# Attention by sketched features, then a Fourier mixer: rows divided as 34c + t, contiguous loads of q, features stationary in k-v, and a new order

## The chip, the cores and the metric

The kernel runs on one core of one Trainium2 chip. Its engines are TensorE (PE, matrix products), VectorE (DVE), ScalarE (ACT), GpSimd (POOL) and SyncE (SP, which here issues the loads and stores). The metric is the device time of one execution in microseconds (us); lower is better. Beside it stands the span of the profiled execution, from its first to its last instruction.

## The reference, cut to what matters

There are 4 batches, 4 heads, 1088 rows, 32 numbers a head. Each row of q and k is turned into 64 features: two projections to 8 numbers each, and all products of the two.

```python
def phi(x):                       # S1, S2: 8 x 32
    a = einsum('rd,bhsd->bhsr', S1, x)
    b = einsum('rd,bhsd->bhsr', S2, x)
    return (a[..., :, None] * b[..., None, :]).reshape(*x.shape[:-1], 64)
q_p, k_p = phi(q), phi(k)
kv = einsum('bhsf,bhsd->bhfd', k_p, v)
z = k_p.sum(axis=2)
x = einsum('bhsf,bhfd->bhsd', q_p, kv) / (einsum('bhsf,bhf->bhs', q_p, z)[..., None] + 1e-6)
x = x.transpose(0, 2, 1, 3).reshape(4, 1088, 128)
mixed = real(fft(fft(x, axis=1), axis=2))
u = x + mixed
un = (u - mean(u)) / sqrt(var(u) + 1e-6)
out = u + maximum(un @ w_ch1, 0) @ w_ch2          # w_ch1: 128 x 512, w_ch2: 512 x 128
```

## The kernel before, in words

The program is a list of named steps. Each step has the engines that may run it, what it reads and writes, and the PSUM banks that it uses. A text, ORDER, gives the order in which the steps are emitted; every engine works its own instructions in that order. ENGINE names the engine of a step that has a choice, and BANK gives the PSUM bank (of eight, 512 float32 columns each) of each use. An entry such as `7@0` in ORDER stands for seven products of a zero tile into bank 0, whose results nobody reads; the text calls them filler products (line 734). There is no scheduler at run time: a step that waits holds up what stands behind it on its engine.

Per batch b the steps are these.

- `ld_k`, `ld_v`, `ld_q`: the loads, issued on SP. k comes as 34 rows a partition, contiguous (4352 bytes); q comes in four loads of 128 KB each, in which a partition gets two neighbouring rows of all four heads (runs of 256 bytes). The 64 rows of a batch that do not fit this pattern come for all batches in five small loads (`ld_qt`).
- `kT`, `kpr`, `kab`, `kp`: k is transposed in 32x32 blocks on VectorE (line 318), projected on TensorE (line 308), copied out of PSUM, and multiplied to features, mostly on POOL (line 77). `kt_pr`, `kt_a`, `kt_p` do the same for the last tile.
- `vc`, `vl`: v is copied beside a column of ones, so that one product gives kv and z.
- `kv`, `kvt`: k-v on TensorE (line 357). v with its ones, 33 columns, is the stationary operand, and the 64 features stream. The result is 33 x 64 a head. `kvc` copies it to SBUF, `kvr` turns it by four products with an identity (line 369), and `kvz` puts it into place as 64 x 33.
- `qT`, `qf`, `qa`, `qp`: q is transposed (line 408) and projected straight to 64 repeated columns of each projection by 16 products of 32 x 64 with 256 columns (line 415). `qa` copies one of the two results (ScalarE, line 70), and `qp` multiplies the two (VectorE, line 426). A step works half a batch and takes four PSUM banks. `qt_T`, `qt_f` (line 437), `qt_a`, `qt_p` do it once for the left-over rows of all batches.
- `pnd`, `den`, `x`: numerator and denominator (line 460), reciprocal, quotient.
- `fo`, `eo`: sums and differences of the two halves and of even and odd parts of x (line 77, on VectorE or POOL).
- `sC`, `sS`: the transform along the rows by products with cosine and sine tables (lines 488 and 492); `zC`, `zS` copy the result out, and `zrC`, `zrS` store it reversed.
- `mix`, `bn`, `sd`, `rc`, `un`, `tr`, `ut`, `ph`, `rl`, `po`, `fin`, `out`: for each half batch g, the transform along the 128 columns, the normalization, a transposition, the two products of the mixer with the relu between them (lines 575 to 597), and the stores. Groups 4 and 9 hold the left-over rows of two batches each.

The tables are made on the chip (`c_iota`, `c_rows`, `c_last`, `t_turn`, `t_ph`, `t_pm`, `t_sin`, `t_cos`, and `t_m...` and `t_again`, which fill in the mirrored part). Batches go in the order 3, 2, 1, 0; the first k is loaded in two parts (`parts`, with `FIRST = 3`).

Of the kernel before, what the change touches and what calls it, by code (L numbers as in the profile page):

```python
# [10 lines left out]
FP32 = mybir.dt.float32  # L11
BF16 = mybir.dt.bfloat16
I32 = mybir.dt.int32
# [10 lines left out]
NM = HALF // 4 + 1  # L24
NF = HALF // 2 + 1
NK = NF + 17
# [27 lines left out]
def program(nc, T, x, bank):  # L54
# [48 lines left out]
    QUARTERS = (1, HALF + 1, S - 256, HALF - 256)  # L103

    def ld_q(b, w):
        nc.sync.dma_start(view(T(f"q_in{b}"), 2 * H * D * w, [[2 * D, H], [1, 2 * D]]),  # L106
                          dram(x["q"], (b * H * S + QUARTERS[w]) * D, [[2 * D, 128], [S * D, H], [1, 2 * D]]))


    def ld_qt(e):  # L110
        for p, n, row, step in ((0, 16, 257, 1), (16, 15, 273, 1), (32, 16, 801, 1), (48, 15, 817, 1)):
            nc.sync.dma_start(view(T("qt_in"), 0, [[D, B * H], [1, D]], p, n),  # L112
                              dram(x["q"], row * D, [[step * D, n], [S * D, B * H], [1, D]]))
        a = T("qt_in")[:]
        pitch = a.ap[0][0]
        nc.sync.dma_start(bass.AP(tensor=a.tensor, offset=a.offset + 31 * pitch, ap=[[32 * pitch, 2], [D, B * H], [1, D]]),
                          dram(x["q"], 0, [[HALF * D, 2], [S * D, B * H], [1, D]]))
    add("ld_qt", "SP", "", "qt_in", ld_qt)
    for b in range(B):
        for i, (lo, n) in enumerate(parts(b)):  # L120
            add(f"ld_k{b}.{i}", "SP", "", f"k_in:{b}/{i}", lambda e, b=b, n=n, lo=lo: ld_k(b, n, lo))
        add(f"ld_v{b}", "SP", "", f"v_in:{b}", lambda e, b=b: ld_v(b))
        for w in range(4):
            add(f"ld_q{b}.{w}", "SP", "", f"q_in:{b}/{w}", lambda e, b=b, w=w: ld_q(b, w))
# [12 lines left out]
    def c_iota(e):  # L137
        nc.gpsimd.iota(T("kk")[:], pattern=[[1, 2], [2, NM]], base=-1, channel_multiplier=0,
                       allow_small_or_imprecise_dtypes=True)
        nc.gpsimd.iota(T("pi")[:], pattern=[[0, 1]], base=0, channel_multiplier=1)  # L140
        nc.gpsimd.iota(T("sr")[:, 0:2], pattern=[[1, 2]], base=1, channel_multiplier=2,
                       allow_small_or_imprecise_dtypes=True)
# [4 lines left out]
    def c_rows(e):  # L147
        nc.vector.tensor_scalar(out=T("sq")[:, 0:2], in0=T("sr")[:, 0:2], scalar1=1.0 / S, scalar2=None, op0=ALU.mult)
# [4 lines left out]
    def c_last(e):  # L153
# [4 lines left out]
        pa, pf, row = T("pa"), T("pf"), T("sr")[:, 2:3]  # L158
        ts(pa[:, 0:1], T("pi")[:], 31, ALU.bitwise_and)
        ts(pa[:, 1:2], T("pi")[:], 32, ALU.bitwise_and)  # L160
        ts(pa[:, 2:3], T("pi")[:], 1, ALU.bitwise_and)
        ts(pf[:, 0:1], pa[:, 0:1], 31.0, ALU.is_equal, -288.0, ALU.mult)
        ts(pf[:, 1:2], pa[:, 0:1], 257.0, ALU.add, pf[:, 0:1], ALU.add)
        ts(row, pa[:, 1:2], HALF / 32.0, ALU.mult, pf[:, 1:2], ALU.add)
        ts(T("sq")[:, 2:3], row, 1.0 / S, ALU.mult)
        ts(T("sg")[:, 0:1], pa[:, 2:3], 2.0, ALU.mult, -1.0, ALU.add)
        ts(T("sg")[:, 1:2], pa[:, 2:3], -2.0, ALU.mult, 1.0, ALU.add)
    add("c_last", "DVE", "iota", "last", c_last)
# [35 lines left out]
    def mirror(e, at, step, n, sign):  # L204
        out = view(T("tab"), at * 2 * NK + NM, [[step * 2 * NK, n], [NK, 2], [1, NM - 1]])
        in_ = view(T("tab"), at * 2 * NK + NM - 1, [[step * 2 * NK, n], [NK - 1, 2], [-1, NM - 1]])
        if isinstance(sign, float) and sign == 1.0:
            copy(e, out, in_)
        elif e == "ACT":
# [12 lines left out]
    add("t_mP", "ACT DVE POOL", "tab:0/S tab:1/C", "tab:m/P", lambda e: mirror(e, 1, 1, 2, 1.0))  # L222
    add("t_mN", "ACT DVE POOL", "tab:0/C tab:1/S", "tab:m/N", lambda e: mirror(e, 0, 3, 2, -1.0))
# [584 lines left out]
```

## Time and profile before

| | us |
|---|---|
| median of 3 runs | 87.29 (86.96 to 87.42) |
| the profiled execution | 87.3 |
| its span | 85.5 |
| TensorE busy | 74.7 |
| VectorE busy | 68.1 |
| ScalarE busy | 55.6 |
| POOL busy | 40.5 |

A row of a group gives the line, the engine, the operation, what it writes and reads, the shape, a count, the busy time and the mean duration of one in ns. A row of a stretch gives the busy time and count of TensorE's products, TensorE's weight loads, VectorE, ScalarE and POOL, then the granted TensorE clock, the share of the DMA engines' time and GB/s. A row of the timeline gives the start, the time from the first start to the last end, and the instructions merged; `[1.24 <-DVE ...]` is idle time before it and what ended it. A float32 product shows as two records on TensorE. Durations of TensorE's products overlap, so the distance from start to start tells what a group holds the engine for. A tile's name stands for all its buffers; `t_k_in` also serves as the buffer of the outputs.

### The profile page before, as it was taken

What the parts mean: (1) busy time and instruction counts of PE and PEld (TensorE: products, weight loads), DVE (VectorE), ACT (ScalarE), POOL (GpSimd) and SP (SyncE); (2) the same over time, 40 slices, a digit from 0 to 9 for tenths busy, and PEclk for the clock granted to TensorE, in tenths of its full rate; (3) what the DMA queues carried; (4) which work ended last, traced back from release to release, by engine and by line L of the source; (5) the groups of instructions that cost most, each with busy time, mean ns of one, the idle gap of its engine ahead of it and who ended that gap; (6) DMA issues with size and microseconds to landing.
All of it is one profiled execution on the core that took longest, in us unless ns stands there. A gap on an engine that the chain in (4) does not pass through costs nothing.

```text
span 85.5 us, 3315 instructions
## 1 busy us (share of the span) xinstructions
PE 74.7 (87%) x1399; PEld 54.2 (63%) x1407; DVE 68.1 (80%) x139; ACT 55.6 (65%) x102; POOL 40.5 (47%) x69
## 2 busy tenths in 40 slices
PE   4999949799987999999999999699899998988800
PEld 1237517798855697846797888376478786855700
DVE  4769495999999759976999598999989889976300
ACT  2637799096915797675493656693768898875720
POOL 6889996069955996799900950360030000000000
PEclk9999999999999999999999999999999999999998
DMA  1896999969999810000000000000033122034061
GB/s 17 175 254 131 314 358 315 280 142 243 270 309 379 212 24 4 8 0 0 0 8 0 8 0 0 8 20 11 0 123 123 45 85 93 30 123 131 22 211 43
DMA packets 14942, 9.65 MB, mean 113 GB/s; under 512 B 10064, under 2 KB 13392, under 8 KB 14928
## 3 DMA queue, kind: packets, MB, share of 16 engines
q1 hardware_dynamic: 14848, 9.44, 39.0%
q8 instruction: 11, 0.18, 1.0%
q14 instruction: 3, 0.02, 0.1%
q10 hardware_dynamic: 80, 0.01, 0.1%
HBM read 7.22 MB, written 2.23 MB: 110 GB/s over the span
## 4 chain that ended last, share of the span: by engine, by line
PE 54%; DVE 18%; DMA 8%; SPq 7%; ACT 5%; issue 3%; ACTq 0%; DVEq 0%
PE ps L357 9%; DMA t_k_in__100<-in_k_dram 8%; PE ps L460 8%; PE ps L597 7%; PE ps L415 7%; PE ps L488 5%; PE ps L575 4%; PE ps L520 3%; PE ps L308 2%; SPq L106 2%; SPq L112 2%; DVE t_v__127 L72 2%; PE ps L492 2%; PE ps L567 2%; PE ps L514 2%
## 5 line engine op out<-in xcount | busy, mean ns | idle before, releaser
L734 PE MATMUL ps<-t_wz 128*128 128x512 bf16 x19 | 7.5, 530 | 1.2 <-DVE t_wz L130 1.2
L70 ACT COPY t_qa__128<-ps 128x1024 f32<-128x1024 f32 x4 | 4.0, 1012 | 4.1 <-PE ps L415 4.1
L734 PEld LDWEIGHTS <-t_wz 128*128 128x128 bf16 x22 | 2.3, 119 | 4.8 <-issue 3.0
L70 ACT COPY t_qa__129<-ps 128x1024 f32<-128x1024 f32 x4 | 4.1, 1013 | 1.2 <-PE ps L415 1.2
L575 PEld LDWEIGHTS <-t_w1b 128*128 128x128 bf16 x40 | 3.3, 97 | 2.5 <-issue 1.0
L590 ACT ACTIVATE t_v_in__101<-ps 128x1024 bf16<-128x1024 f32 x4 | 4.0, 1022 | 0.4 <-PE ps L575 0.4
L415 PE MATMUL ps<-t_qT__116,t_sa 32*64 32x256 f32 x64 | 2.9, 400 | 1.4 <-DVE t_qT__116 L408 1.2
L77 POOL TENSOR_TENSOR t_e__140<-t_x__136 128x512 bf16<-128x512 bf16 x2 | 2.3, 1159 | 4.0 <-DVE t_x__136 L471 4.0
L590 ACT ACTIVATE t_v_in__102<-ps 128x1024 bf16<-128x1024 f32 (+1 forms) x4 | 3.6, 918 | 0.7 <-PE ps L575 0.7
L575 PE MATMUL ps<-t_unT__164,t_w1b 128*128 128x512 bf16 (+1 forms) x15 | 3.6, 335 | 0.3
L77 POOL TENSOR_TENSOR t_kp__121<-t_ab__117 128x512 f32<-128x512 f32 x2 | 2.1, 1066 | 3.5 <-ACT t_ab__117 L70 3.5
L590 ACT ACTIVATE t_v_in__104<-ps 128x1024 bf16<-128x1024 f32 x3 | 3.0, 1016 | 1.0 <-PE ps L575 0.8
L590 ACT ACTIVATE t_v_in__103<-ps 128x1024 bf16<-128x1024 f32 x3 | 3.0, 1028 | 0.8 <-PE ps L597 0.8
L415 PE MATMUL ps<-t_qT__115,t_sa 32*64 32x256 f32 x64 | 3.0, 400 | 0.5 <-DVE t_qp__132 L426 0.5
L460 PE MATMUL ps<-t_kvz,t_qp__130 128*64 128x66 f32 x96 | 3.4, 224 | 0.0
L460 PE MATMUL ps<-t_kvz,t_qp__131 128*64 128x66 f32 x96 | 3.4, 223 | 0.0
L460 PEld LDWEIGHTS ps<-t_kvz,t_qp__130 128*64 128x64 f32 x96 | 3.0, 138 | 0.5 <-DVE t_kvz L72 0.4
L460 PEld LDWEIGHTS ps<-t_kvz,t_qp__131 128*64 128x64 f32 x96 | 3.1, 138 | 0.4 <-ACT t_tab L193 0.4
L77 POOL TENSOR_TENSOR t_e__139<-t_x__135 128x512 bf16<-128x512 bf16 x1 | 1.2, 1151 | 4.4 <-DVE t_x__135 L471 4.4
L597 PE MATMUL ps<-t_w2b,t_v_in__102 128*128 128x128 bf16 x36 | 2.5, 219 | 0.7 <-ACT t_v_in__102 L590 0.7
L70 ACT COPY t_k_in__98<-ps 128x512 f32<-128x512 f32 (+1 forms) x4 | 2.0, 504 | 1.5 <-PE ps L597 1.5
L415 PEld LDWEIGHTS ps<-t_qT__116,t_sa 32*64 32x64 f32 x64 | 1.1, 130 | 2.9 <-DVE t_qT__116 L408 1.7
(318 smaller groups left out, 263.2 us busy)
## 6 DMA issues: line engine op xcount, KB each, us to landing
out_dram<-t_k_in__100 SPq DMA_DIRECT2D x6, 128.0 KB, 2.1
out_dram<-t_k_in__98 SPq DMA_DIRECT2D x6, 128.0 KB
t_v_in__104<-in_v_dram SPq DMA_DIRECT2D x1, 544.0 KB
t_k_in__100<-in_k_dram SPq DMA_DIRECT2D x1, 544.0 KB
t_k_in__99<-in_k_dram SPq DMA_DIRECT2D x1, 544.0 KB
t_v_in__103<-in_v_dram SPq DMA_DIRECT2D x1, 544.0 KB
t_v_in__102<-in_v_dram SPq DMA_DIRECT2D x1, 544.0 KB
t_k_in__98<-in_k_dram SPq DMA_DIRECT2D x1, 544.0 KB
```

What stands on the lines that cost most here:

```text
L70: nc.scalar.copy(out, in_)
L72: nc.vector.tensor_copy(out, in_)
L77: (nc.vector if e == "DVE" else nc.gpsimd).tensor_tensor(out=out, in0=in0, in1=in1, op=op)
L357: nc.tensor.matmul(ps(f"kv{b}", 64 * (h // 2), [[1, F]], 64 * (h % 2), 33), v, w, start=(b, h % 2) not in begun, stop=True, tile_position= ...
L415: nc.tensor.matmul(ps(f"q{b}.{w}", 512 * g + 256 * f, [[1, 256]], 64 * h, 64), view(T(src), 0, [[1, F]], 32 * g, 32), view(T(f"qT{b % 2}") ...
L460: nc.tensor.matmul(ps(f"nd{b}", 512 * (s // 3) + 132 * (s % 3) + 66 * pr, [[1, 66]], 64 * h, 64), q, view(T("kvz"), 2 * KP * b + KP * pr, ...
L488: nc.tensor.matmul(ps(f"z{trig}{b}", 512 * c, [[1, NK]]), T(f"eo{b % 2}")[:, trig, c, t, :], T("tab")[:, t, trig, NK * c:NK * c + NK], sta ...
L520: nc.tensor.matmul(ps(u, 256 * w + 128 * t, [[1, 128]]), zcol(b, trig, half, first(half, w) + t, 2, 128), m, start=False, stop=True, skip_ ...
L575: nc.tensor.matmul(ps(use, 128 * n * i, [[1, 128 * n]]), T("w1b")[:, 128 * c:128 * c + 128], T(f"unT{g % 3}")[:, 0:128 * n], start=True, s ...
L590: nc.scalar.activation(out=out, in_=in_, func=ACT.Relu)
L597: nc.tensor.matmul(ps(u, 128 * t, [[1, 128]]), ht_view(g, 512 * c + 128 * t, [[1, 128]]), T("w2b")[:, c, :], start=False, stop=True, skip_ ...
L734: nc.tensor.matmul(made["ps"][:, at, :], made["wz"][:, 0:128], made["wz"][:], start=True, stop=True)
```

## The change

The 1088 rows of a head are divided as 34c + t: c is one of 32 partitions and t one of 34 places, so that 128 partitions hold the four heads of a batch. A batch of q is then one load with 4352 contiguous bytes a partition (for batch 3 two loads of half a partition each). The rows left over are the multiples of 17, t = 0 and t = 17; they come with the same load, so the five loads of `ld_qt` go, and `qt_T` is a small step for each batch, `qt_f`, `qt_a` and `qt_p` one for every two batches. The left-over tile's product in `pnd` is a step of its own, `pnt`.

Since a partition now holds rows of one head, the transposed q has head h on the 32 partitions from 32h on. The projection products follow: `tile_position` is (32h, 64(h mod 2)) instead of (32g, 64h) over four g and two h.

The tables have their columns in the order of the tiles, so that a tile of the transform is read with steps of two columns, rows are 273 columns instead of 290, and `c_tab` and `t_again` go. k-v has the 64 features stationary and v with its ones streaming, so its result is 64 x 33 at once; `kvc`, `kvr` and the identity `c_idf` go. ORDER, BANK and ENGINE are new: batches go in the order 0, 1, 2, 3, with 16 filler products instead of 22. The two split loads of k still belong to batch 3. The stores of the left-over rows are one instead of five.

```diff
-NM = HALF // 4 + 1
-NF = HALF // 2 + 1
-NK = NF + 17
+NM = 128 + 17
+NK = NM + 128
...
-    QUARTERS = (1, HALF + 1, S - 256, HALF - 256)
-    def ld_q(b, w):
-        nc.sync.dma_start(view(T(f"q_in{b}"), 2 * H * D * w, [[2 * D, H], [1, 2 * D]]),
-                          dram(x["q"], (b * H * S + QUARTERS[w]) * D, [[2 * D, 128], [S * D, H], [1, 2 * D]]))
+    def qparts(b):
+        return ((0, TT), (TT, TT)) if b == FIRST else ((0, 2 * TT),)
+    def ld_q(b, lo, n):
+        nc.sync.dma_start(view(T(f"q_in{b}"), lo * D, [[1, n * D]]),
+                          dram(x["q"], (b * H * S + lo) * D, [[2 * TT * D, 128], [1, n * D]]))
...
-                nc.tensor.matmul(ps(f"kv{b}", 64 * (h // 2), [[1, F]], 64 * (h % 2), 33), v, w,
+                nc.tensor.matmul(ps(f"kv{b}", 33 * (h // 2), [[1, 33]], 64 * (h % 2), 64), w, v,
...
-    def qT(b, half):
-        nc.vector.transpose(view(T(f"qT{b % 2}"), 512 * half, [[1, 512]]), view(T(f"q_in{b}"), 512 * half, [[1, 512]]))
+    def qT(b, w):
+        out = [[1, 8], [-256, 2], [8, 32]] if w == 0 else [[1, 8], [256, 2], [8, 32]]
+        nc.vector.transpose(view(T(f"qT{b % 2}"), (256, 512)[w], out), view(T(f"q_in{b}"), (1, 18)[w] * D, [[1, 16 * D]]))
...
     def qfeat(b, w):
-        for g in range(4):
-            for h in range(2):
+        for i in range(2):
+            for h in range(H):
                 for f, src in enumerate(("sa", "sb")):
                     nc.tensor.matmul(
-                        ps(f"q{b}.{w}", 512 * g + 256 * f, [[1, 256]], 64 * h, 64),
-                        view(T(src), 0, [[1, F]], 32 * g, 32),
-                        view(T(f"qT{b % 2}"), 512 * w + 64 * h, [[128, 2], [256, 2], [1, 64]], 32 * g, 32),
-                        start=True, stop=True, tile_position=(32 * g, 64 * h), skip_group_check=True)
+                        ps(f"q{b}.{w}", 512 * (2 * (h // 2) + i) + 256 * f, [[1, 256]], 64 * (h % 2), 64),
+                        view(T(src), 0, [[1, F]], 32 * h, 32), view(T(f"qT{b % 2}"), 512 * w + 256 * i, [[1, 256]], 32 * h, 32),
+                        start=True, stop=True, tile_position=(32 * h, 64 * (h % 2)), skip_group_check=True)
...
+    def qt_T(b):
+        nc.vector.transpose(view(T(f"qtT{b // 2}"), 64 * (b % 2), [[1, 2], [2, 32]]), view(T(f"q_in{b}"), 0, [[TT * D, 2], [1, D]]))
+    def qt_f(i):
+        for h in range(H):
+            for f, src in enumerate(("sa", "sb")):
+                nc.tensor.matmul(
+                    ps(f"qt{i}", 512 * (h // 2) + 128 * f, [[1, 128]], 64 * (h % 2), 64), view(T(src), 0, [[1, F]], 32 * h, 32),
+                    view(T(f"qtT{i}"), 0, [[1, 128]], 32 * h, 32),
+                    start=True, stop=True, tile_position=(32 * h, 64 * (h % 2)), skip_group_check=True)
...
 ORDER = """
+c_wz c_iota ld_q0.0 c_bias c_rows d_turn c_last d_ph d_pm c_kvz c_v12 c_mask c_eye16 t_turn2 c_vt c_v11 ld_s c_v10
+c_idb c_cen t_ph2 c_rev 7@0 s_t qT0.0 s_use 5@1 qf0.0 d_trig t_sin2 t_turn1 ld_k0.0 t_pm2 t_cos2 t_turn0 kT0.0 1@4
+kpr0 t_mC qa0.0 ld_k1.0 kab0 ld_v0 kp0.0 qT0.1 kT1.0 kp0.3 kp0.1 kt_pr0 3@6 kpr1 qp0.0 kt_a0 t_ph1 ld_q1.0 qt_T1 qt_T0
+qf0.1 vl0 ld_v1 ld_k2.0 vc0.0 vc0.1 qa0.1 kt_p0 qt_f0 kv0.0 kab1 kvt0 kv0.3 t_ph0 qT1.1 qp0.1 kv0.1 ld_q2.0 ld_w1
...
 BANK = dict(w.split("=") for w in """
+st=0 w1=6 k0=4 kt0=5 kv0=5 k1=4 kt1=4 kv1=0 k2=4 kt2=5 kv2=7 k3=7 kt3=7 kv3=7 qt0=6 qt1=4 q0.0=0 q0.1=0 nd0=5 z00=2
...
```

## The prediction

> **What bounds the kernel now.** I read the busy times of the page first, then each engine's busy time by stretch, then who made TensorE wait, then the chain that ended last.
>
> ```profile
> span 85.5 us, 3315 instructions
> PE 74.7 (87%) x1399; PEld 54.2 (63%) x1407; DVE 68.1 (80%) x139; ACT 55.6 (65%) x102; POOL 40.5 (47%) x69
> ...
> 6.50:16.00 9.50, 7.78 (x171) 5.21 (x172) 7.49 (x12) 7.40 (x14) 7.42 (x14) 1.00 0.99 287
> 16.00:52.50 36.50, 35.20 (x917) 28.31 (x918) 32.03 (x53) 23.67 (x48) 24.94 (x25) 1.00 0.38 101
> 52.50:81.40 28.90, 26.37 (x305) 18.99 (x305) 24.53 (x52) 21.32 (x35) 2.97 (x3) 1.00 0.18 60
> ```
>
> The first number after a stretch's length is TensorE's busy time. From 6.5 to the end of its last product at 81.3 it is busy 7.78 + 35.20 + 26.37 = 69.35 us and idle about 5.4: 1.7 before 16.0, 1.3 up to 52.5, 2.4 behind that. So TensorE is the bound, and a change of its work counts almost one to one; what other engines save counts only through those 5.4 us. The waits behind them (total, times, longest):
>
> ```profile
> PE ps L415 <- DVE t_qT__116 L408: 1.2, 1, 1.2
> ...
> PE ps L597 <- ACT t_v_in__102 L590: 0.7, 1, 0.7
> PE ps L369 <- ACT t_kvs__151 L70: 0.6, 1, 0.6
> PE ps L415 <- DVE t_qp__132 L426: 0.5, 1, 0.5
> ```
>
> The chain that ended last gives its first 14.6 us to load issues and one load,
>
> ```profile
> 6.95 0.51 SPq L106
> ...
> 7.50 7.11 DMA t_k_in__100<-in_k_dram
> ```
>
> which overstates the loads: TensorE works through most of that time.
>
> **The change part by part: q features (the term that decides).** q arrives in contiguous runs, so transposing its 32x32 blocks puts head h on partitions 32h and up. Before, every row group held rows of all heads, and the 16 products of a feature step sat on eight places of the array (four row groups times two column halves), two on each. Now head h can only use row group h with column half h mod 2: four places, four products on each. What four places cost is in this trace, because the step for the left-over rows (line 437) uses exactly four: its eight products, half as many as line 415 has, take nearly as long.
>
> ```profile
> 6.58 0.73 PE L415 MATMUL ps<-t_qT__116,t_sa 32*64 32x256 f32 x16
> 7.07 0.68 PE L415 MATMUL ps<-t_qT__116,t_sb 32*64 32x256 f32 x16
> 7.68 1.15 PE L308 MATMUL ps<-t_sblk,t_kT__110 128*64 128x64 f32 x32
> 8.66 0.26 PE L323 MATMUL ps<-t_sblk,t_kT__110 128*64 128x32 f32 x4
> 8.85 0.68 PE L437 MATMUL ps<-t_qtT,t_sa 32*64 32x256 f32 x8
> 9.33 0.63 PE L437 MATMUL ps<-t_qtT,t_sb 32*64 32x256 f32 x8
> 9.89 1.47 PE L734 MATMUL ps<-t_wz 128*128 128x512 bf16 x5
> ```
>
> (A float32 product shows as two records.) Line 415: 32 records from 6.58 to 7.68, 1.10 us. Line 437: 16 records from 8.85 to 9.89, 1.04 us. The time goes by rounds on one place, not by products: four rounds each. The second pair of rounds starts 0.48 us after the first (6.58 to 7.07, 8.85 to 9.33), so a round is at most 0.24 us; four 512-column bf16 products on the full array, the same amount of streaming, give the lower end:
>
> ```profile
> 78.07 1.02 PE L575 MATMUL ps<-t_unT__164,t_w1b 128*128 128x512 bf16 x4
> 78.93 1.06 PE L597 MATMUL ps<-t_w2b,t_v_in__103 128*128 128x128 bf16 x16
> ```
>
> 0.86 for four. A feature step will have eight rounds: four more, 0.86 to 0.96, less some ramp. I take +0.8 (0.7 to 0.9), nearest the 437 row: 1.04 + 0.86 = 1.90 against 1.10. Eight steps: **+6.4 us** (5.6 to 7.2). The Trainium skill, page "TensorEngine Tiling (Array Packing)", section Tiling Modes, lists eight tiles for 32x64 and calls tiles independent; the trace agrees (16 records on four places take 1.04 us, 32 on eight 1.10).
>
> **k-v with features stationary.** The copy of k-v out of PSUM and the re-transposing products (line 369) go, four times each. The k-v products now stream 33 columns instead of 64.
>
> ```profile
> 34.28 0.64 PE L357 MATMUL ps<-t_kp__120,t_v__126 128*33 128x64 f32 x16
> 34.75 0.62 PE L357 MATMUL ps<-t_kp__124,t_v__126 128*33 128x64 f32 x16
> ...
> 40.82 0.42 PE L369 MATMUL ps<-t_idf,t_kvs__152 33*64 33x33 f32 x8
> 41.17 0.73 PE L415 MATMUL ps<-t_qT__115,t_sa 32*64 32x256 f32 x16
> ```
>
> Line 369 holds TensorE 0.35 us: **-1.4 us** for four. The copies were 0.5 us on ScalarE or VectorE, and their latency is the 0.6 us wait of the list. For the streaming, the bounds are half of line 357's 0.47 for 16 records (288 records in all, 8.5 us, so -4.2) and nothing. The nearest row is line 369 itself, which streams 33 columns against 64 stationary ones: 0.35 for 8 records, against 0.235 for 8 of line 357, so shorter streams show no gain. I take **0**, with +0.3 as the other end (64 stationary columns to load instead of 33). The skill's same page, section Instruction Overhead, says that a short stream costs like one of 60 columns, though its section on swapping advises the swap; by the first the term is 0, by column counts -4. The trace sides with the first.
>
> **Tables.** Rows of 290 columns become 273.
>
> ```profile
> L488 PE MATMUL ps<-t_tab,t_eo__142 128*128 128x290 bf16 x16 | 2.6, 288 | 0.0
> ```
>
> Two such groups and a third as much on line 492, some 7 us in all, times 17/290 is 0.4 at most: **-0.3**. Fewer set-up instructions on POOL and VectorE (c_idf, c_tab, t_again gone; four small ones more in c_rows) lie beside the 12 filler products, and cost nothing unless s_use slips past 6.5.
>
> **Left-over rows.** One feature step becomes two of half the width, and the last tile's product a step of its own: a second ramp and some switches, **+0.4** (0 to 0.8).
>
> **Filler products.** Of ten behind the first twelve, four remain.
>
> ```profile
> 6.50:16.00 9.50, 1.96 (x7) 0.70 (x8) 1.00 0.99 287
> 16.00:52.50 36.50, 0.39 (x1) 0.11 (x2) 1.00 0.38 101
> ```
>
> These are line 734's: 2.35 us, so four cost 0.9: **-1.4**. The granted clock is 1.00 in both stretches; TensorE will idle less, so I expect no slower clock.
>
> **Loads and new order.** Batch 0 comes first, unsplit. What is now a load of 544 KB:
>
> ```profile
> 4.00 0.71 DVE L408 STREAM_TRANSPOSE t_qT__116<-t_q_in__108 128x512 f32<-128x512 f32 x1 [0.27 <-DMA t_q_in__108<-in_q_dram]
> 14.63 1.31 DVE L318 STREAM_TRANSPOSE t_kT__109<-t_k_in__100 128x1088 f32<-128x1088 f32 x1 [0.87 <-DMA t_k_in__100<-in_k_dram]
> ```
>
> Two quarters, 256 KB, had landed by 4.0; 288 KB more at the 287 GB/s of the stretch is 1.0, so q0 is there by 5.0, k0 1.9 later at 6.9, k1 at 8.8. The first feature step starts where it did, near 6.6, when s_use is done, and ends near 8.6; k0's transpose (1.3) ends at 8.3 under it. The next gate is new: k1's projection shares PSUM bank 4 with k0's, so it waits for the copy kab0, queued on ScalarE behind qa0.0.
>
> ```profile
> 7.92 1.01 ACT L70 COPY t_qa__128<-ps 128x1024 f32<-128x1024 f32 x1 [0.44 <-PE ps L415]
> 8.88 0.58 ACT L70 COPY t_ab__118<-ps 128x512 f32<-128x512 f32 x1
> ```
>
> 8.6 + 1.0 + 0.6 = 10.2; k0's projection, its left-overs and three fillers carry TensorE to about 10.7. So the 1.7 us of early idle should go: **-1.7**. In the middle the k-v wait goes (-0.6) and the longer feature steps give the other engines more cover: with each step's duration from this trace, on the engine that the new list gives it, VectorE has some 5 us less to do, ScalarE about the same, POOL 6 more. I leave 0.3 of 1.3: **-1.0**. On SP, 28 issues replace 40; q of batch 3, split in two, goes behind w1, v2 and v3, and is not needed for another 20 us. The left-over rows leave in one store in place of five, before the last stores. At the end batch 3 comes last, and its four folds run in series on POOL,
>
> ```profile
> L77 POOL TENSOR_TENSOR t_e__140<-t_x__138 128x512 bf16<-128x512 bf16 x2 | 2.3, 1160 | 0.0
> ```
>
> 4.6 us between x3 and its transform rows, which about 7 us of mixer work have to cover; then rows, evictions, reversal and mixers follow one another as before. I keep **2.4**, today's idle there (1.0 to 4.0).
>
> **Sum.** TensorE's true work 69.35 - 2.35 = 67.0; + 6.4 - 1.4 - 0.3 + 0.4 = 72.1; with fillers 73.0; idle 0 + 0.3 + 2.4 = 2.7. 6.6 + 73.0 + 2.7 = 82.3 against 81.3: +1.0. What follows the last product stays, a copy of 0.6 us and its stores:
>
> ```profile
> 80.21 1.07 PE L597 MATMUL ps<-t_w2b,t_v_in__104 128*128 128x128 bf16 x16 [0.22 <-ACT t_v_in__104 L590]
> ...
> 81.31 0.58 ACT L70 COPY t_k_in__98<-ps 128x512 f32<-128x512 f32 x1 [0.69 <-PE ps L597]
> ```
>
> The profiled execution took 87.30 us, the median of the runs is 87.29. **88.3 us**, slower by 1%.
>
> **Rivals.** *Idle almost vanishes (ends faster or level).* The work grows by 3.6 net of fillers (69.35 to 73.0), the idle is 5.4: the sign turns at an idle of 1.7. For it: the lighter load of VectorE, on which two of the four listed waits hang. Idle 0.5 to 1.7 gives 86.1 to 87.3, 86.7 in the middle. Against it: 2.4 us of today's idle sit in the tail, where the chain from bn to relu remains. *The idle stays.* The in-order engines meet a feature step 0.8 us longer eight times, qa and qp behind it hold four banks, and POOL takes more copies: 4.0 to 6.0 us idle, 89.6 to 91.6, 90.7. *The extra rounds do not appear, or streaming 33 columns halves k-v.* 88.3 - 6.4 = 81.9 or 88.3 - 4.2 = 84.1; lines 437 and 369 speak against.
>
> **How the numbers follow.** A difference under 0.5% (0.4 us) can hardly be told from none. Chances: forecast 0.45 (87.3 to 89.6), idle vanishes 0.27, idle stays 0.20, rounds or k-v cheap 0.08. Faster: all of the last and two thirds of the second, 0.25; same: the rest of the second and the forecast's lowest part, 0.16; slower 0.59. Range: the work's bounds (5.6 to 7.2 on the features) and idle from 1 to 5 give 86.0 to 91.0; the forecast alone 87.3 to 89.6.
>
> **What would show it.** Right: feature steps hold TensorE 1.8 to 2.0 us each with eight rounds; TensorE busy 77 to 79 in all; no line 369; k-v groups still near 0.47 for 16 records; first k projection by 9; idle from 6.5 to 16 under 0.5. Wrong: feature steps near 1.1 us, k-v groups near 0.25, or idle in the tail under 1 or over 4.

## The result and the profile after

The changed kernel takes 91.71 us (91.52 to 93.97, four runs) against 87.21 us before (86.96 to 87.42): a ratio of 1.051, 95% interval 1.047 to 1.055. The forecast was 88.3 us, 1% slower; it is 5% slower, outside the forecast's own 87.3 to 89.6 and outside the widest range of 86.0 to 91.0. The profiled execution took 91.52 us, its span is 89.7 us, 4.2 more than before. Some executions of most versions are disturbed, which means 1.5% or more above the fastest of the same version; where they spread a version's times widely, its undisturbed ones are named.

Page of the changed kernel, then its stretches (length, then busy time of TensorE's products, weight loads, VectorE, ScalarE, POOL; clock, DMA share, GB/s), cut at the first feature product and behind the last product:

```profile
span 89.7 us, 3227 instructions
PE 78.6 (88%) x1379; PEld 58.9 (66%) x1385; DVE 64.2 (72%) x130; ACT 56.7 (63%) x101; POOL 46.3 (52%) x73
...
DMA packets 6142, 9.65 MB, mean 108 GB/s; under 512 B 624, under 2 KB 3952, under 8 KB 6128
...
7.06:16.00 8.94, 8.78 (x186) 6.92 (x187) 8.94 (x13) 6.03 (x11) 6.35 (x8) 1.00 1.03 398
16.00:52.50 36.50, 34.46 (x763) 27.29 (x760) 26.03 (x39) 21.66 (x42) 27.33 (x29) 1.00 0.16 53
52.50:84.60 32.10, 30.81 (x433) 23.23 (x434) 24.37 (x54) 25.11 (x44) 7.44 (x9) 1.00 0.20 53
```

TensorE is still the bound. From its first feature product to its last product it is busy 8.78 + 34.46 + 30.81 = 74.05 us and idle 3.5 (0.1 of it behind the last product). In the forecast's terms the span of 89.7 us is 7.06 + 74.05 + 3.4 + 5.2 (from the last product's end at 84.5 to the end of the span), where the forecast had 6.6 + 73.0 + 2.7 + 4.2. Four terms, each too small: start by 0.46, work by 1.05, idle by 0.7, tail by 1.0.

The work. A feature step and the k-v groups behind it, from the timeline:

```profile
35.36 0.68 PE L383 MATMUL ps<-t_qT__114,t_sa 32*64 32x256 f32 x8
35.84 0.63 PE L383 MATMUL ps<-t_qT__114,t_sb 32*64 32x256 f32 x8
36.27 0.67 PE L383 MATMUL ps<-t_qT__114,t_sa 32*64 32x256 f32 x8
36.70 0.67 PE L383 MATMUL ps<-t_qT__114,t_sb 32*64 32x256 f32 x8
37.31 0.66 PE L337 MATMUL ps<-t_v__126,t_kp__122 128*64 128x33 f32 x16
37.80 0.64 PE L337 MATMUL ps<-t_v__126,t_kp__123 128*64 128x33 f32 x16
```

The step holds TensorE from 35.36 to 37.31, 1.95 us, where it was 1.10. (All eight steps together go from 8.81 to 15.43 us, counted from start to start without idle time.) A k-v group of 16 records takes 0.49 with 33 streamed columns, where 64 took 0.47.

The waits of TensorE, in total, times, longest:

```profile
PE ps L267 <- DMA t_s<-in_S_dram: 1.4, 1, 1.4
PE ps L433 <- issue: 1.3, 1, 1.3
...
PE ps L461 <- DVE t_qp__130 L393: 0.4, 1, 0.4
PE ps L304 <- issue: 0.4, 1, 0.4
```

Two of the rows shown are marked "issue": TensorE stood still and the profile shows nothing that it waited for. The longer one is in the middle of a group that had begun:

```profile
22.04 0.34 PE L433 MATMUL ps<-t_kvz,t_qp__130 128*64 128x66 f32 x5
23.71 0.97 PE L433 MATMUL ps<-t_kvz,t_qp__130 128*64 128x66 f32 x26 [1.33 <-issue]
```

Nothing like it is among the waits before. The end, SP's last issues, of the changed kernel:

```profile
84.41 1.19 SPq L579 DMA_DIRECT2D out_dram<-t_k_in__95  x2
85.68 1.21 SPq L579 DMA_DIRECT2D out_dram<-t_k_in__94  x2
```

and of the kernel before:

```profile
80.66 0.83 SPq L608 DMA_DIRECT2D out_dram<-t_k_in__100  x2
81.92 0.81 SPq L608 DMA_DIRECT2D out_dram<-t_k_in__98  x2
```

A pair of stores now takes 1.2 us to issue, where it took 0.8. Before, a store wrote 256 rows in one run; now it writes 16 groups of 16 rows, 34 rows apart, and its pattern has one level more. Which of the two costs the time was not tested. The store of the left-over rows (line 583), with rows 17 apart but one level less and half the bytes, took 0.34 us to issue. The last copy ended at 85.14, but its stores had to wait on SP for the pair ahead of them.

### The profile page after: what moved, and what is told of

Read it like the earlier page. It is cut to its first block, busy times and chain, and to the rows that moved or that the text cites. A ratio compares the mean times of both kernels' runs of the same rounds, so it can differ in the third digit from the quotient of the medians.

```text
span 89.7 us, 3227 instructions
## 1 busy us (share of the span) xinstructions
PE 78.6 (88%) x1379; PEld 58.9 (66%) x1385; DVE 64.2 (72%) x130; ACT 56.7 (63%) x101; POOL 46.3 (52%) x73
## 4 chain that ended last, share of the span: by engine, by line
PE 70%; ACT 8%; DVE 6%; DMA 5%; issue 4%; ACTq 1%; DVEq 0%
PE ps L383 17%; PE ps L337 11%; PE ps L433 8%; PE ps L568 6%; PE ps L546 5%; DMA t_s<-in_S_dram 5%; PE ps L289 4%; PE ps L461 4%; PE ps L494 3%; PE ps L699 2%; ACT t_v_in__96 L561 2%; ACT t_v_in__98 L561 2%; PE ps L487 2%; PE ps L465 2%; PE ps L538 2%
## 5 line engine op out<-in xcount | busy, mean ns | idle before, releaser
L699 PE MATMUL ps<-t_wz 128*128 128x512 bf16 x15 | 5.4, 496 | 1.3 <-DVE t_eps L125 1.2
L383 PE MATMUL ps<-t_qT__114,t_sa 32*64 32x256 f32 x64 | 5.4, 395 | 0.0
L383 PE MATMUL ps<-t_qT__115,t_sa 32*64 32x256 f32 x64 | 5.4, 395 | 0.0
L383 PE MATMUL ps<-t_qT__114,t_sb 32*64 32x256 f32 x64 | 5.2, 374 | 0.0
L383 PE MATMUL ps<-t_qT__115,t_sb 32*64 32x256 f32 x64 | 5.2, 374 | 0.0
L73 POOL COPY t_zr__148<-t_z__144 128x546 bf16<-128x546 bf16 x2 | 1.3, 640 | 7.0 <-DVE t_z__144 L71 6.6
L561 ACT ACTIVATE t_v_in__96<-ps 128x1024 bf16<-128x1024 f32 x4 | 3.9, 1020 | 0.4 <-PE ps L494 0.4
L699 PEld LDWEIGHTS <-t_wz 128*128 128x128 bf16 x16 | 1.6, 114 | 3.5 <-issue 1.8
L383 PEld LDWEIGHTS ps<-t_qT__114,t_sa 32*64 32x64 f32 x64 | 2.3, 130 | 1.9 <-ACT t_kvz L69 0.8
L76 POOL TENSOR_TENSOR t_eo__140<-t_e__138 128x512 bf16<-128x512 bf16 x3 | 3.5, 1152 | 0.1
L76 POOL TENSOR_TENSOR t_eo__141<-t_e__139 128x512 bf16<-128x512 bf16 x3 | 3.4, 1153 | 0.1
L561 ACT ACTIVATE t_v_in__98<-ps 128x1024 bf16<-128x1024 f32 x3 | 3.0, 1021 | 0.7 <-POOL t_e__139 L76 0.6
```

Of the source, the lines that this page charges most:

```text
L76: (nc.vector if e == "DVE" else nc.gpsimd).tensor_tensor(out=out, in0=in0, in1=in1, op=op)
L383: nc.tensor.matmul(ps(f"q{b}.{w}", 512 * (2 * (h // 2) + i) + 256 * f, [[1, 256]], 64 * (h % 2), 64), view(T(src), 0, [[1, F]], 32 * h, 32 ...
L561: nc.scalar.activation(out=out, in_=in_, func=ACT.Relu)
L699: nc.tensor.matmul(made["ps"][:, at, :], made["wz"][:, 0:128], made["wz"][:], start=True, stop=True)
```

## The experiments

Every kernel below was timed beside the kernel before, which stood at 86.55 to 87.39 us (medians).

### Is it the number of rounds on a place?

**e1_eight**: both factors of a feature on eight places; the first factor then lies on the wrong half of the partitions and two copies on ScalarE bring it back.

```diff
-                        ps(..., 512 * (2 * (h // 2) + i) + 256 * f, [[1, 256]], 64 * (h % 2), 64),
+                    half = h % 2 if f else 1 - h % 2
+                        ps(..., 512 * (h // 2 + 2 - 2 * f) + 256 * i, [[1, 256]], 64 * half, 64),
...
-        copy(e, T(f"qa{w}")[:], ps(f"q{b}.{w}", 0, [[512, 4], [1, 256]]))
+        for p in range(2):
+            copy(e, view(T(f"qa{w}"), 0, [[1, 1024]], 64 * p, 64), ps(f"q{b}.{w}", 1024, [[1, 1024]], 64 - 64 * p, 64))
```

> The changed kernel with its feature products on eight places again: the first factor of a head goes to the other column half, and the copy of it to SBUF is two copies of 64 partitions that bring it back (one more ScalarE instruction of about 1.0 us a step). If the eight rounds of a feature step make the slowdown, a step holds TensorE 1.1 us instead of 1.95, TensorE's busy time falls from 78.6 to about 72, and the time from 91.7 to between 85 and 88. If the slowdown comes from waits in the new order instead, the freed time turns into idle and the time stays above 90.

89.54 us (88.84 to 90.59), ratio 1.028 (1.019 to 1.038). A step holds TensorE 0.92 us where products of the same tile shape follow (14.94 to 15.86 in its timeline) and 1.05 where others do. TensorE's busy time falls to 75.7 us, not to about 72, and the time is above the expected 85 to 88 and just below the rival's 90. ScalarE's busy time rises by 8.0 to 64.7 us, for a copy of 64 partitions takes as long as one of 128 (1.006 us each, 16 of them):

```profile
L69 ACT COPY t_qa__127<-ps 64x1024 f32<-64x1024 f32 x8 | 8.0, 1006 | 4.8 <-PE ps L384 4.7
```

**e2_eight_split**: the same, one of the two copies on VectorE (`copy(("ACT", "DVE")[p], ...)`).

> As the run before, but of the two copies one is on ScalarE and one on VectorE, so that the product behind them waits 1.0 to 1.2 us, not 2.0. If the latency of the copies holds back what the eight places give, this is 1 to 2 us faster than two copies on ScalarE; if TensorE's work is what counts, the two are within 0.5 us of one another.

99.42 us, the slowest of the versions with eight places: a loss of some 9 us against e1, where a gain of 1 to 2 or none was expected. The copy stands in VectorE's queue until TensorE has finished the step, and the transpositions of k behind it are late:

```profile
PE ps L289 <- DVE t_kT__109 L299: 4.0, 2, 2.5
PE ps L337 <- DVE t_ktp__112 L309: 2.2, 1, 2.2
```

**e6_eight_free**: eight places, one straight copy and no bringing back, so ScalarE and VectorE do what they do in the changed kernel. What it leaves out is the right pairing: it multiplies factors of different heads.

```diff
-        copy(e, T(f"qa{w}")[:], ps(f"q{b}.{w}", 0, [[512, 4], [1, 256]]))
+        copy(e, T(f"qa{w}")[:], ps(f"q{b}.{w}", 1024, [[1, 1024]]))
```

> The changed kernel with the two factors of the features on eight places of the array and nothing that brings the first factor back to the second one's partitions: the product pairs factors of different heads, so the computation is changed on purpose there, with the same instructions on VectorE and ScalarE as in the changed kernel. The theory of rounds: each of the eight feature steps takes 0.9 to 1.1 us instead of 1.95, TensorE's work falls by 7 to 8 us, and since VectorE and ScalarE have 25 us of room the time falls by 5 to 7.5: 84 to 86.7. The rival, that the other engines' chains set the pace once the features are short: the idle time of TensorE rises by what the steps save, 88 to 90.

Of ten runs (86.04 to 89.75) five are undisturbed, with a median of 86.40: 5.2 us under the changed kernel, inside the expected 84 to 86.7, and about level with the kernel before (ratio 0.992, 0.986 to 0.998). A step with a product of another shape behind it holds TensorE 1.05 us. In the profiled execution (88.47, one of the disturbed) the last product ends at 79.31 where it ended at 84.52, which is the same 5.2 us, though the first feature product came only at 8.03; what that execution took longer lies behind its last product. So the rounds make the loss, and the rest of the change is worth about nothing.

**e8_before_eight_rounds**: the other way round, in the kernel before, each feature step's loop run twice (`for g in (0, 1, 2, 3) * 2`), the places in turn.

> The kernel before with the whole loop of each feature step run twice over the same eight places (the second pass writes the same values again), so eight rounds of products for every place instead of four, with the places in turn and never more than two products of a place in a row. The theory of rounds: a step takes 1.95 to 2.0 us instead of 1.10, TensorE's work rises by 6.8 to 7.2, of which the fillers and the idle time give back up to 2.5: 91 to 93.5. The rival, that the longer step of the changed kernel comes from its tile shape or its operands and not from the number of rounds: under 88.5. If products of one place in a row are what made the earlier doubling so slow, this one does not show it.

96.77 us (96.48 to 97.22), ratio 1.110. More than expected. One step:

```profile
20.77 0.73 PE L415 MATMUL ps<-t_qT__115,t_sa 32*64 32x256 f32 x16
21.25 0.68 PE L415 MATMUL ps<-t_qT__115,t_sb 32*64 32x256 f32 x16
...
22.36 0.79 PE L415 MATMUL ps<-t_qT__115,t_sb 32*64 32x256 f32 x14
23.08 1.10 PE L460 MATMUL ps<-t_kvz,t_qp__131 128*64 128x66 f32 x30
```

2.31 us instead of 1.10. The first four rounds take 0.9 as ever, the other four 1.4. So eight rounds make the step longer with tile shape and operands as before. But 0.36 us a step above the changed kernel's 1.95 stay unexplained (the second loop overwrites the first one's results); with them, this run shows that more rounds cost time, and not that they alone make the 1.95.

**e5_before_double**: an earlier try at the same, each product twice in a row, so four in a row for a place (`tuple(enumerate(("sa", "sb"))) * 2`).

> The kernel before, each feature product done twice on its place, so eight rounds a step as in the changed kernel, and nothing else touched. If rounds on a place make TensorE's time and TensorE is the bound, the time rises by 4.5 to 6.8 us, to 91.7 to 94. If other engines cover the longer steps, it stays under 90.

193.79 us. This doubled nothing cleanly: a feature step takes over 10 us, its 64 records run nearly one after another, and the granted clock falls.

```profile
6.33:16.90 10.57, 10.57 (x64) 6.84 (x64) 2.71 (x5) 1.17 (x4) 3.08 (x8) 0.78 1.01 288
```

With two products in a row for a place (before, and e8) eight places work at once; with four in a row they do not. How far TensorE looks past a product whose place is busy was not measured. The Trainium skill, page "TensorE: Matmul & The Clock Gate", Part 2, says that products stay in program order and only weight loads are pulled ahead; that places fall idle behind a busy one agrees with it, and the loss here is a factor of nearly ten, where the work only doubled.

### Is it the start?

**e4_early**: S loaded first on SP's queue, `s_use` ahead of `qT0.0`.

```diff
-c_wz c_iota ld_q0.0 c_bias ...
+c_wz c_iota ld_s ld_q0.0 c_bias ...
-... s_t qT0.0 s_use 5@1 qf0.0
+... s_t s_use qT0.0 5@1 qf0.0
```

> The changed kernel with the load of S issued first, ahead of the first load of q on SP's queue, and s_use run ahead of what it waits behind on VectorE. The start theory: S no longer lands behind the large loads, the first feature step starts at about 6.6 us instead of 7.06, and the whole kernel is 0.3 to 0.5 us faster (91.2 to 91.4). The rival, that the first step is held by something else (the cosine table, or the first transposition of q, which now lands later): no change, 91.5 to 92.

91.76 us (91.59 to 91.97): no change. S came early, but q came later, and TensorE, idle meanwhile, went on at a lower clock (the row of the page in tenths, slices of 2.25 us):

```profile
PE ps L383 <- DVE t_qT__114 L376: 1.6, 1, 1.6
...
PEclk9996699999999999999999999999999999999997
```

**e13_start**: S as it was, `qT0.0` ahead of `t_ph2` on VectorE.

> The changed kernel with qT0.0 ahead of t_ph2 on VectorE, the load of S as it was. In the earlier trial with S first, q landed later and the first product waited for qT0.0 instead. The start theory: qT0.0 runs from about 4.7 to 5.8 us, s_use follows S (landed at 5.7) at 5.85 to 6.3, the first feature step starts at 6.3 to 6.45 instead of 7.06, and the time falls by 0.5 to 0.7 us: 91 to 91.3. The rival, that the start is taken back in later waits: 91.6 to 92.

91.91 us: no change. `s_use` ended at 6.37, but the first product came at 8.03, since the five filler products took 2.31 us instead of 1.25, at a granted clock shown as 1.00:

```profile
5.79 2.31 PE L699 MATMUL ps<-t_wz 128*128 128x512 bf16 x5
```

The fillers of e1, e2, e6, e8 and e10 were as slow, those of the changed kernel, e3, e4, e11 and e12 were not. Idle time ahead of them does not tell the two apart: 2.31 us stand behind 1.24 us of idle time here, 1.25 behind 1.35 in the changed kernel and behind 2.19 in e12, and in the kernel before they took 2.15 with none. There is one trace of each kernel, so whether the pace belongs to the kernel or to the execution is open. The same page of the Trainium skill, Part 1, has half the clock in the default state and full clock only after some 3.4 us of work, in a window that runs freely; a pace of almost half agrees with it, but the row of the granted clock does not show it.

The first feature product came 0.97 us later than in the changed kernel, and still the last one ended at 84.47 instead of 84.52: the stop at 22.38 is gone from this trace, and with it what the start had lost. So the start and the stops are not separate terms.

**e14_start3**: S on SP and the first q on ScalarE's queue at the same time, both steps ahead of `t_ph2`, eight fillers instead of five so that TensorE is not idle.

```diff
-... t_ph2 c_rev 7@0 s_t qT0.0 s_use 5@1 qf0.0
+... c_rev 7@0 s_t s_use qT0.0 t_ph2 8@1 qf0.0
```

> The changed kernel with S loaded first on SP's queue and the first part of q on ScalarE's at the same time, s_use and qT0.0 ahead of t_ph2 on VectorE, and eight fillers instead of five ahead of the first feature step so that TensorE is not idle there. The start theory: the first feature step starts at 6.2 to 6.5 us instead of 7.06, at the full clock, and the time falls by 0.4 to 0.8: 91 to 91.4, unless a stop for a late block grows by the same amount. The rival, that TensorE then waits for the blocks of its program instead (the second one comes at about 21 us whatever the start): the stop at matmul 349 grows to about 2 us and the time is 91.5 to 92.

91.19 us (90.66 to 91.77), 0.4 to 0.5 less by the medians, with runs that overlap the changed kernel's. The first feature step starts at 6.59 instead of 7.06, but TensorE goes on behind the longer stop at 23.45 instead of 23.71, the shorter stop grew from 0.35 to 0.5, and the last product ends at 84.37 instead of 84.52. The stop at matmul 349 did not grow to 2 us (it is 1.0), so the rival's number is wrong; its mechanism is half right, for most of the earlier start is taken back there. So in this order the start is worth at most half a microsecond.

### Is it the tail?

**e3_tail**: one of the last two stores on ScalarE's queue.

> The changed kernel, with one of the last two stores issued on ScalarE's queue, idle by then. If the last stores are late because they stand behind the two stores of the group before on SP and because each issue now takes 0.6 us, the span falls by 0.5 to 1.0 us (91.7 to 90.7 to 91.2). If the landing itself is slower for the new pattern of rows, it falls by 0.2 or less.

92.55 us, but 90.83 to 93.1, with one undisturbed run (90.83, 0.7 under the changed kernel's profiled 91.52): a single run, so the time cannot tell. The trace can: from the last product's end (84.31) to the end of the span are 4.7 us instead of 5.2.

**e7_eight_free_early_tail**: e6 with the load of S first, `s_use` ahead of `qT0.0` and this store.

> The last kernel with S loaded first and one of the last two stores on ScalarE's queue. If the loss is the sum of rounds, start and tail, the terms add up: 0.4 us for the start and 0.5 to 0.8 for the tail below the last kernel, 83 to 85.7, which is below the kernel before. If the start and the tail are only noise: the same as the last kernel within 0.3.

85.89 us (85.65 to 87.32), 0.5 under e6's undisturbed 86.40, less than the expected 0.9 to 1.2 and just above the expected 83 to 85.7. The earlier start gained nothing: the first product came at 7.15 instead of 8.03, but the last one ends at 79.37 instead of 79.31. The largest wait is now a stop for nothing, and TensorE goes on behind it at 23.28, in e6 at 23.23:

```profile
PE ps L434 <- issue: 2.2, 1, 2.2
```

So the gain is the tail's: 4.74 us behind the last product here, as in e3.

### What are the stops that wait for nothing?

In the changed kernel and in those variants that have them they stand at the same products, counted from the start: number 221 or 222 and number 349. With the weight loads these are TensorE's instructions 449 and 705, 256 apart. (The doubled kernel before, e8, has one of 1.42 us at instruction 1217, twice 256 further on.) The packets of the queue for instructions come in blocks of 16 KB. From the records of products and packets, in us:

```
kernel   second block's packet   TensorE stops at 349   from packet's end
after        21.08 - 22.12          22.38 - 23.71             1.59
e3           20.97 - 22.10          22.45 - 23.50             1.40
e14          20.85 - 22.00          22.45 - 23.45             1.45
e7           20.59 - 21.67          21.05 - 23.28             1.61
e11          20.17 - 21.28          20.96 - 22.80             1.52
```

TensorE goes on 1.4 to 1.6 us after the packet, wherever it stopped. The stop ahead of it fits as well (17.24 behind a packet that ended at 15.86 in the changed kernel), and so does e8's (1.5 behind its packet). When the block is fetched varies: 632 of TensorE's instructions had started by then in the changed kernel, 512 in e15 below. By these figures the stop is a late block of TensorE's own program.

**e10_gates**: the loads from w1 on let go in three portions, by one-element writes on POOL to a tile of each portion (`g_w1`, `g_v3`, `g_k3`), so that SP waits there.

> The changed kernel with its loads let go in three portions: one-element writes on POOL to the first tile of a portion, after kp0.2, kp1.2 and kp2.2, make SP wait there, so that the loads of w1 and of batches 2 and 3 do not all stand in the DMA queues from 10 us on. The theory of the late instructions: TensorE's stops inside a group with nothing to wait for (1.33 and 0.35 us in the changed kernel, always at matmul 349 and 221 to 222, 128 matmuls apart) are blocks of its program that come in late because the loads stand ahead of them; with the loads apart the second block comes at about 18 to 19 us instead of 21.08, the stop at matmul 349 is under 0.3 us, and the time falls by 0.8 to 1.4 us: 90.3 to 91. The rival, that a block is fetched late for a reason of its own: the stop stays, 91.5 to 92.

In this kernel and in e12 the load of batch 3's k was put behind the step that transposes it, so batch 3 is computed with the k of batch 0. 92.41 us (91.47 to 94.33): no gain. The stop at 349 is gone and the second block came at 19.30, but S landed late and the fillers were slow, so the first product came at 8.90, and a new wait for `qp` cost 0.56. Not a clean test.

**e15_start3_gates2**: e14 with the portions, in order, and the last ones let go earlier.

```diff
-... ld_q2.0 ld_w1 ld_v2 ld_v3 ld_q3.1 kt_pr1 ld_k3.1 ld_k3.0 ld_q3.0 kp0.2 ld_w2 kp1.1
+... ld_q2.0 kt_pr1 kp0.2 g_w1 ld_w1 ld_v2 kp1.1
-... kp1.3 kp1.2 qf1.1
+... kp1.3 kp1.2 g_k3 ld_k3.0 ld_q3.1 ld_k3.1 ld_q3.0 qf1.1
-... kT3.0 kvz1 kp2.1 kp2.2
+... kT3.0 kvz1 kp2.1 g_v3 ld_v3 ld_w2 kp2.2
```

> The last kernel with the loads let go in three portions (w1 and v of batch 2 after kp0.2; k and q of batch 3 after kp1.2; v of batch 3 and w2 after kp2.1). The theory of the late instructions: no stop at matmul 349 over 0.3 us, the second block fetched at 17.5 to 19.5 us, and the time 1.2 to 2 us below the last kernel: 89.2 to 90.2. The rival, that the stop is paid back as waits for VectorE and ScalarE: within 0.5 of the last kernel.

90.27 us (89.81 to 91.88), 0.9 under e14 (1.0 by undisturbed runs). Its waits have no stop over 0.2:

```profile
PE ps L701 <- DVE t_eps L127: 1.2, 1, 1.2
PE ps L463 <- DVE t_qp__130 L395: 0.4, 1, 0.4
PE ps L540 <- ACT t_v_in__98 L563: 0.3, 1, 0.3
```

The second block came at 18.01. The gain is smaller than expected; in the profiled execution the eight fillers took 2.73 us where e14's took 1.90, and the first product came at 7.37 instead of 6.59. Even so the last product ended at 82.63, 1.7 us ahead of e14's. So in this order the late block goes when the loads do not all stand in the queues at once, and it is worth 1 us or a little more. In what way loads hold up a block that has a queue of its own is not shown, and loads alone do not do it: in the kernel before they run on until 30.8 us, and its blocks come 2 us or more ahead of need, while e8, with the same loads, has a late one.

### A version that beats both

Of each head the first row tile can go to its usual half of the columns and the second to the other one. Both factors then lie on the same partitions, all eight places are used, and the second row tile is multiplied with a second copy of kvz whose halves are exchanged.

```diff
-                        ps(..., [[1, 256]], 64 * (h % 2), 64),
+                        ps(..., [[1, 256]], 64 * ((h + i) % 2), 64),
...
     def kvz(b, e):
-        for h in range(2):
-            copy(e, view(T("kvz"), 2 * KP * b + 33 * h, [[KP, 2], [1, 33]], 64 * h, 64), ...)
+        for x in range(2):
+            for h in range(2):
+                copy(e, view(T("kvz"), 2 * KP * (B * x + b) + 33 * h, [[KP, 2], [1, 33]], 64 * (h ^ x), 64), ...)
...
-                                     view(T("kvz"), 2 * KP * b + KP * pr, [[1, 66]]), ...
+                                     view(T("kvz"), 2 * KP * (B * (s % 2) + b) + KP * pr, [[1, 66]]), ...
```

> A version that computes the reference with eight places: of each head the first row tile goes to its usual half of the array's columns and the second to the other half, both factors to the same one, and the second row tile is multiplied with a second copy of kvz that has the two heads' halves exchanged (two small copies a batch more on ScalarE, 0.43 us). With qT0.0 ahead of t_ph2 and one of the last two stores on ScalarE's queue. The theory of rounds with the measured terms: the eight-place kernel with wrong pairs and these two terms took 85.9; the second kvz copies cost 0 to 0.8: 85.5 to 86.7, under the kernel before by 0 to 1.5. The rival, that the copies of kvz sit on the path to each numerator product: 87 to 88.5.

One of four executions is undisturbed, 85.81, inside the expected 85.5 to 86.7; the others reach 89.36. It stops 1.83 us at matmul 349.

> The last kernel with the loads let go in three portions. In the eight-place kernel with wrong pairs the stops of TensorE that wait for nothing were 2.2 and 0.6 us. The theory of the late instructions: these go to under 0.6 in sum and the time falls by 1.5 to 2.2 us below the last kernel, 83.5 to 85. The rival, that the blocks come late anyway: the same as the last kernel within 0.4.

85.77 us (85.51 to 85.89). Here too batch 3 is computed with the k of batch 0. There is no stop over 0.2 us that waits for nothing, but 1.33 us of waiting for `qp`, behind late loads of batch 3, took its place. The time is e11's within 0.4, the rival's number, but not by its mechanism: no block came late.

> The eight-place version with the exchanged kvz, the start of the last two kernels and one of the last two stores on ScalarE's queue, loads as in the changed kernel. Theory: as the earlier eight-place version (85.8 in its undisturbed runs) less 0 to 0.7, with a stop at matmul 349 of about 2 us: 85 to 86. The rival, that the start decides and no block is late: 84 to 85.

86.91 us (86.47 to 87.63, ten runs): above both ranges. In the profiled execution (87.42, at a granted clock of 0.963) the stops are 0.6 and 0.7; new is a wait of 1.5 us for `kT0.0`, since the earlier first step ends before k is transposed.

> The last kernel with the loads let go in three portions. The theory of the late instructions: 1.2 to 2.2 us below the last kernel, 83.2 to 84.5, with no stop over 0.3 us that waits for nothing. The rival, that waits for VectorE take its place (1.33 us in the earlier version with portions): 85 to 86.

85.37 us (85.12 to 86.89), ratio to before 0.981 (0.973 to 0.990), 1.5 under e17: the gain that the theory gave, but a time in the rival's range. In the profiled execution (86.89, at a granted clock of 0.964) the stop at 349 is gone, one of 0.4 and waits of 1.7 and 1.3 for `kT0.0` and for `kab3` remain. Against e15 it is 4.9 us less, with eight places, the second kvz that they need and the store of e3 as the only differences.

**e18_best**: e16 with `t_ph2` behind `kT0.0`, three fillers instead of one there, the tables' steps behind `kab0`, batch 3's k let go after `kp1.0`.

> The eight-place version with the loads in portions, with t_ph2 after kT0.0 on VectorE and the tables' steps that follow it after kab0 on ScalarE, three fillers instead of one before the first k projection, and the loads of batch 3's k let go after kp1.0 instead of kp1.2. If the two waits (1.66 us for kT0.0 and 1.27 us for ab of batch 3) are a matter of order, the time falls by 1 to 2 us: 83.4 to 84.5. The rival, that VectorE's and ScalarE's own work sets the pace there, or that the earlier loads hold up the third block of TensorE's program: within 0.5 of the last one, 85 to 85.8.

84.55 us (84.27 to 85.42, six runs), ratio to before 0.974 (0.968 to 0.980): at the upper end of what the theory gave and below the rival's range. The feature step and the waits:

```profile
22.91 0.73 PE L386 MATMUL ps<-t_qT__115,t_sa 32*64 32x256 f32 x16
23.39 0.68 PE L386 MATMUL ps<-t_qT__115,t_sb 32*64 32x256 f32 x16
24.01 0.66 PE L339 MATMUL ps<-t_v__125,t_kp__118 128*64 128x33 f32 x16
...
PE ps L702 <- DVE t_eps L127: 1.2, 1, 1.2
PE ps L291 <- DVE t_kT__108 L301: 1.2, 1, 1.2
PE ps L291 <- DVE t_kT__109 L301: 0.7, 1, 0.7
```

1.10 us a step, as before the change, and no wait of TensorE marked "issue" among those of 0.2 us or more. The wait for `kab3` is gone; that for `kT0.0` is 1.2 us still.

## Why the prediction was wrong

The direction and the deciding mechanism were right. All four terms of the sum came out higher than forecast: start by 0.46, work by 1.05, idle by 0.7, tail by 1.0, which is 3.2 us of span together. The steps that failed are the start's condition, the left-over rows, the idle time left for the middle, and the stores of the tail. The work is counted here from start to start with idle time left out, so that overlaps are not counted twice.

- **Feature steps, +0.8 each, +6.4.** Right in mechanism: a step goes by rounds on one place, as line 437 said. e6 and e18 confirm it, and e1 and e8 agree. Measured 15.43 - 8.81 = +6.6 for all eight, so mis-sized by 0.2 and inside its bounds.
- **k-v, streaming 33 columns: 0.** Right: 9.86 us in all against 9.82. (The busy times, 10.8 of line 337 against 10.3 of line 357, differ because they count overlaps.) The re-transposition is gone, -1.4. Exchanging the streaming and the stationary operand gained nothing.
- **Left-over rows, +0.4 (0 to 0.8).** Failed: +0.9, past its upper bound and about half of what the work missed. The numerator products take 9.4 us where they took 8.7, now that the last tile's product is a step of its own, and line 405 takes 1.3 where 437 took 1.0.
- **Tables -0.3, fillers -1.4.** Near: lines 461 and 465 take 7.4 us where 488 and 492 took 7.7, and the fillers behind the first feature step fell from 2.1 to 0.8, -1.3. The left-over rows of k (line 304) cost 0.2 more, which no term had.
- **"The first feature step starts where it did, near 6.6, when s_use is done."** Failed, +0.46. The condition was named (unless s_use slips past 6.5) and it did slip, to 7.00. The forecast timed the arrival of q and k, and left out S and what stands in VectorE's queue. S, whose load was not touched, lands behind 544 KB loads (its last packet ends at 4.98 instead of 2.67). But it was not the last to come: the product that `s_use` reads ran from 5.71 to 5.91. VectorE was behind: a step of the tables waited for POOL until 5.17, and the transposition of q behind it takes 1.11 us with a strided output instead of 0.71:

```profile
5.17 0.52 DVE L175 SCALAR_TENSOR_TENSOR t_ph<-t_kk,t_sr,t_ph 128x290 f32<-128x290 f32 x1 [0.48 <-POOL t_ph L171]
5.61 1.11 DVE L376 STREAM_TRANSPOSE t_qT__114<-t_q_in__100 128x512 f32<-128x512 f32 x1
6.55 0.22 DVE L272 TENSOR_TENSOR t_sblk<-ps,t_mask 128x64 f32<-128x64 f32 x1
```

  With `qT0.0` and `s_use` ahead of that step (e13), `s_use` was done at 6.37. Start and middle are not separate terms, though: in e7 and e14 the late blocks took most of an earlier start back.
- **Early idle to 0.** Right: 0.16 us from 7.06 to 16. k1's projection came without a wait, as worked out; the first k projection at 9.33 was 0.3 past its mark.
- **"I leave 0.3 of 1.3" in the middle.** Failed: 2.0 us. The k-v wait did go, and VectorE (-3.9), ScalarE (+1.1) and POOL (+5.8) came near the estimates, but 1.7 us of stops for late blocks of TensorE's program are new. No row before had one, and the forecast had none; it took the quicker loads as a gain only. e15, without these stops, is 1.0 us faster than e14.
- **Tail idle 2.4.** Too much: 1.2 up to the last product's end. The rival in which idle vanishes was half right, in this place only.
- **"What follows the last product stays."** Failed, +1.0: the last stores wait 0.5 for SP and their issue takes 0.4 longer. The store's new row pattern was in the diff, and its issue time was never priced.
- **Range and rivals.** The bounds named for the work and the idle add up to 85.8 to 91.4, not 86.0 to 91.0; the time lies outside both. It lies at the upper end of "the idle stays" (89.6 to 91.6), but not by its mechanism: idle fell from 5.4 to 3.5. That rounds do not appear is refuted.

## What to carry to other kernels

Count the products that one place of the array has to take, not the products: a layout that ties a head to one row group and one column half took the step from 1.10 to 1.95 us, and with the two halves used by different row tiles it was 1.10 again. When loads become large and early, look at all that shares the queues with them: the small load that everything waits for, and the engine's own program. An earlier start is worth nothing if a later gate takes it back. Price the tail's stores by their pattern, for here nothing hid them.

## What the runs showed of the hardware that was not expected

- TensorE stops for blocks of its own program: at its instructions 449, 705 and (e8) 1217, for 0.3 to 2.2 us, until 1.4 to 1.6 us after the 16 KB packet; with the loads in portions the stops were gone in e15 and e18.
- Products in a row for one place: with one in a row a feature step took 1.05 us (e6), with two 1.10 (before, e18), with four over 10, in part by a granted clock of 0.78 (e5).
- Five fillers took from 1.25 to 2.31 us, in no order with the idle time ahead of them, with the granted clock shown as 1.00 in the changed kernel and in e13 alike.
- A transposition on VectorE took 1.11 us with a strided output instead of 0.71; a store's issue took 0.6 us instead of 0.4 when its rows lay in 16 groups and its pattern had one level more.
